# Cutting the 127-row transfers at a sequence's head into 15 and 112 rows, in a backward kernel of two convolutions and a joint network

## The chip, the cores and the metric

The kernel runs on one core of a Trainium2 chip. The time of a run is the device time in microseconds (us). Before the change it was 840.08 us, the median of three runs (835.29 to 840.89). Executions of one kernel scatter here by some 10 us, and a few before runs fell in a slow state (850 to 854 us); comparisons below use the fast runs alone.

Five engines matter. TensorE (PE) multiplies, busy 95% of the span before the change. ScalarE (ACT) and VectorE (DVE) empty its results, busy 88% and 90%. GpSimd (POOL) issues loads through a software queue (on the page of before, q0 software_dynamic, 54.07 MB). SyncE (SP) issues stores and transposing transfers through a hardware queue (q1 hardware_dynamic, 116.45 MB), one after another; "SPq" in a profile is that engine issuing a transfer. The page gives the time of the transfers as a share of 16 DMA engines: 24.9% for q0, 68.2% for q1.

## The reference

```python
def _fwd_reference(x, w1, w2, g, w_f, w_g, w_o):      # x: 2 x 16000 x 256, bf16
    h = gelu(conv(x, w1, K=3))[:, ::2, :]
    f = gelu(conv(h, w2, K=3))[:, ::2, :]             # 2 x 4000 x 256
    fe, ge = f @ w_f, g @ w_g                         # g: 2 x 8 x 256
    j = tanh(fe[:, :, None, :] + ge[:, None, :, :])
    return j @ w_o                                    # 2 x 4000 x 8 x 256

def reference(x, w1, w2, g, w_f, w_g, w_o, grad_out):
    _out, _vjp = jax.vjp(forward, x, w1, w2, g, w_f, w_g, w_o)
    return (_out, *_vjp(grad_out))                    # the output, and a gradient for each input
```

The convolutions are written shorter here than in the original. The output in question is the gradient of x, 2 x 16000 x 256.

## The kernel before

The 2 x 4000 positions after both convolutions are worked off in chunks of up to 512. Four rows of x belong to one position, so a block of 128 positions is stored with 128 partitions of four rows of 256 bf16, 2,048 bytes each. This grid is shifted by three rows against the sequence: the first partition of the first block of a sequence has only one valid row. It is handled alone, and 127 partitions remain.

The two queues, and the helper by which each transfer is issued (all transfers therefore have lines 329 or 331 in a profile; the tile's name tells them apart):

```python
LOADQ, STOREQ = "POOL", "SP"
HR_AT = (0.7, 0.4, 0.3)
    # ... cut ...
    def dma(q, out, in_, r, w, bytes_, new=(), transpose=False, at=None, after=(), cost=None, hold=(), nb=None):
        def go(e):
            eng_ = nc.sync if e == "SP" else nc.gpsimd if e == "POOL" else nc.scalar
            if transpose:
                return eng_.dma_start_transpose(out=out(), in_=in_())
            else:
                return eng_.dma_start(out=out(), in_=in_())
        c = 1260.0 if transpose else 400.0 if q == "SP" else cost or (750.0 if q == "POOL" else 100.0)
        return op(q, c, go, r=r, w=w, new=new, at=at, after=after, hold=hold, nb=nb,
                  work=bytes_ / 256 * 1.25 if transpose else bytes_ / 300.0)
```

The load of x rows for the weight gradient, tile `X` in the profile, from POOL's software queue:

```python
    def load_x5(b, s0, m, at, hold=()):
        X5 = buf("x5", [P, 5, D], BF16, "X5")
        r0, r1 = (1, m) if s0 == 0 else (0, m)
        if s0 + m - 1 == MQ:
            r1 = m - 1
        src = x[b, 0:1, :]
    # ... cut ...
            dma(LOADQ, lambda: X5[:].rearrange("p f d -> p (f d)")[r0:r1],
                lambda: bass.AP(tensor=src.tensor, offset=src.offset + (4 * (s0 + r0) - 3) * D,
                                ap=[[4 * D, r1 - r0], [1, 5 * D]]),
                r=[], w=[(X5, "m")], bytes_=(r1 - r0) * 2560, new=new, at=at, hold=hold, cost=550.0)
        return X5
```

The store of the gradient of x, tile `GX_SB`, on the sync engine's hardware queue:

```python
            s0, m = c0 + bl * P, min(P, Ws - bl * P)
            r0, r1 = (1 if s0 == 0 else 0), (m - 1 if s0 + m - 1 == MQ else m)
            dst = out_1[b, 0:1, :]
            if r0 == 1:
                dma(STOREQ, lambda: out_1[b, 0:1, :], lambda GX=GX: GX[0:1, 3, :], r=[(GX, 1)], w=[], bytes_=512, cost=550.0)
            if r1 > r0:
                dma(STOREQ, lambda s0=s0, r0=r0, r1=r1, dst=dst: bass.AP(
                    tensor=dst.tensor, offset=dst.offset + (4 * (s0 + r0) - 3) * D, ap=[[4 * D, r1 - r0], [1, 4 * D]]),
                    lambda GX=GX, r0=r0, r1=r1: GX[:].rearrange("p c d -> p (c d)")[r0:r1], r=[GX], w=[],
                    bytes_=(r1 - r0) * 2048, cost=550.0)
```

On the same sync queue lie the output's stores (tile `OUT_SB`, six buffers), the transposing loads of `grad_out` (tile `GOT`) and eight transposing copies for each chunk (two each of the tiles `HRo`, `HRs`, `FR` and `HRe`):

```python
    def load_got(g_, u, at):
        b, ci, c0, W = chunks[g_]
        GOT = buf("got", [P, KT, CW], BF16, "GOT")
        dma("SP", lambda: GOT[:, :, :W], lambda: grad_out[b, c0:c0 + W, u, :], r=[], w=[GOT], bytes_=W * D * 2, new=[GOT],
            transpose=True, at=at)
    # ... cut ...
        for kt in range(KT):
            dma("SP", lambda kt=kt: R[:, kt, 0:Wp // P, :], lambda kt=kt: SRC[:, kt, off:off + Wp],
                r=[(SRC, kt)] + [(SRC, k) for k in keys], w=[(R, kt)], bytes_=Wp * P * 2, new=[R] if kt == 0 else [],
                transpose=True, nb=nb)
    # ... cut ...
        late = [start_of[g_] + HR_AT[2] * W] * 2 if g_ < 2 else [t0 + HR_AT[0] * dt, t0 + HR_AT[1] * dt]
        dma_rows("HRo", "hro", g_, HTo, 2, ["z"], late[0])
        dma_rows("HRs", "hrs", g_, HTo, 1, ["h", "z"], late[0])
        dma_rows("HRe", "hre", g_, HTe, 0, ["z"], late[1])
        dma_rows("FR", "fr", g_, FT, 0, ["z"], late[0])
```

PE makes a block of output, ACT or DVE copies it from its accumulator into an `OUT_SB` buffer, the sync queue stores it, and only when the store has landed is the buffer free again; the six are used in turn. A list scheduler with a cost model (`Flow`) fixes the order of instructions on each engine when the kernel is built.

## Time and profile before

| | before |
|---|---|
| three timed runs | 835.29 to 840.89, median 840.08 us |
| profiled run, span | 847.4 us (this run was in the slow state) |
| PE busy | 803.3 us, 95% |
| PE dry in batch 0, at 118.9 us | 8.65 us, then 1.30 |
| 127-row store, batch 1 | holds 15.86 us of the chain |

From the profile's page of before: the span, busy time of each engine with its share and number of instructions, and the engines' shares of the chain of work that ended last.

```profile
span 847.4 us, 17952 instructions
...
PE 803.3 (95%) x6428; PEld 595.2 (70%) x6428; DVE 763.5 (90%) x1730; ACT 749.6 (88%) x1207; POOL 182.6 (22%) x391
...
PE 68%; ACT 12%; DVE 9%; DMA 7%; issue 2%; SPq 1%; ACTq 0%; DVEq 0%; POOL 0%
```

PE is the bound: it is busy 95% of the span and holds 68% of the chain. A change that moves only transfers can gain only where PE waits for something. Two such places have a 127-row store in front of them.

The sync queue's timeline of before in batch 0. Columns: start in us, us that the issue took, engine, line, operation, destination<-source, count.

```profile
102.83 0.75 SPq L331 DMA_DIRECT2D out_dram<-GX_SB  x2
103.67 9.95 SPq L329 DMA_TRANSPOSE GOT<-in_grad_out_dram  x1
113.71 1.11 SPq L331 DMA_DIRECT2D out_dram<-GX_SB  x1
114.88 3.07 SPq L329 DMA_TRANSPOSE HRo<-HTo  x2
118.05 2.70 SPq L329 DMA_TRANSPOSE HRs<-HTo  x2
120.79 3.40 SPq L329 DMA_TRANSPOSE FR<-FT  x2
124.28 0.53 SPq L331 DMA_DIRECT2D out_dram<-OUT_SB  x1
```

The two `GX_SB` stores (1 row and 127 rows) are issued in 0.75 us together. The next instruction is a transpose of `grad_out` (tile `GOT`). The median of the 144 in this profile is issued in 1.27 us; this one holds the queue for 9.95 us, the longest of all. Everything behind it is late, and the next `OUT_SB` store comes only at 124.28.

What the DMA engines did meanwhile, from the stretch table of before. Columns: stretch, its length, busy us and instructions of PE, PEld, DVE, ACT and POOL, granted PE clock, DMA share, GB/s. (The DMA share is a mean over the 16 engines and comes out above 1 in some stretches; only its low, flat values are read here.)

```profile
105.00:110.00 5.00, 5.00 (x37) 3.21 (x36) 4.81 (x11) 5.00 (x10) 0.72 (x1) 1.00 2.34 95
110.00:115.00 5.00, 5.00 (x47) 4.10 (x44) 5.00 (x12) 5.00 (x8) 0.72 (x1) 1.00 0.07 26
115.00:120.00 5.00, 3.93 (x25) 2.21 (x23) 3.09 (x8) 1.08 (x2) 0.57 (x1) 1.00 0.54 167
120.00:125.00 5.00, 0.00 (x0) 0.00 (x0) 0.00 (x0) 0.00 (x0) 0.00 (x0) 0.85 1.30 184
125.00:130.00 5.00, 1.11 (x3) 0.36 (x3) 0.84 (x2) 3.05 (x6) 0.00 (x0) 0.50 0.89 235
```

From 110 to 115 us the core moves 26 GB/s at a DMA share of 0.07, about what one engine of sixteen, busy all the time, would make (an estimate: 1/16 = 0.0625). The next stretches show the consequence: no engine computes from 120 to 125 us, and the granted clock then falls to 0.50.

ACT's and PE's timelines of before, the instructions after the waits ("dry" below means that an engine has nothing that it can start). The brackets give the idle time before an instruction and what ended it.

```profile
126.95 0.58 ACT L314 CAST OUT_SB<-ps 128x512 bf16<-128x512 f32 x1 [10.86 <-DMA out_dram<-OUT_SB]
```

```profile
127.58 1.01 PE L306 MATMUL ps<-GOT,WT 128*128 128x512 bf16 x2 [8.65 <-ACT OUT_SB L314]
129.90 1.01 PE L306 MATMUL ps<-WO,JT 128*128 128x256 bf16 x4 [1.30 <-DVE g_s L436]
```

ACT waits 10.86 us for a store of an `OUT_SB` buffer to land, and PE waits 8.65 us for ACT. In batch 1 the same store shows in the chain of before (start, us, what), and in the list of waits from 500 to 540 us (who waited for what: us, times, longest):

```profile
511.20 15.86 DMA out_dram<-GX_SB
```

```profile
ACT GX_SB L316 <- DMA out_dram<-GX_SB: 4.3, 1, 4.3
...
DVE GX_SB L321 <- DMA out_dram<-GX_SB: 3.0, 1, 3.0
```

There the buffer that runs out is `GX_SB` itself, and the wait is shorter.

### The profile page before, as it was taken

How to read it: one execution, taken by the hardware profiler on the slowest of the kernel's cores; microseconds unless marked ns; L12 is line 12 of the kernel's file. 1: busy time of each engine (PE TensorE's matmuls, PEld its weight loads, DVE VectorE, ACT ScalarE, POOL GpSimd, SP SyncE). 2: the span in 40 equal slices, each digit the busy share in tenths (PEclk: the TensorE clock that was granted, in tenths of full speed). 3: DMA queues.
4: the chain of work that ended last, by engine and by line, in shares of the span. 5: the costliest groups of instructions: out<-in, count | busy, mean ns of one | idle time of the engine just before them, and what ended most of it. 6: DMA issues, size and time to landing. Idle time of an engine off the chain costs nothing.

```text
span 847.4 us, 17952 instructions
## 1 busy us (share of the span) xinstructions
PE 803.3 (95%) x6428; PEld 595.2 (70%) x6428; DVE 763.5 (90%) x1730; ACT 749.6 (88%) x1207; POOL 182.6 (22%) x391
## 2 busy tenths in 40 slices
PE   7589969999999999999999999999999999999995
PEld 5356646677686767877777677576776867788984
DVE  5699958998999989998989998898989999998983
ACT  6789949999899998988899997998898999988762
POOL 5021201212112121233131212112121121214121
PEclk9899998999999999999999999999999999999999
DMA  9989999998979896986899999999999797958452
GB/s 203 162 174 218 213 123 246 248 238 218 249 184 259 199 242 157 237 213 185 200 167 236 230 233 115 221 229 248 210 250 243 182 276 158 255 146 204 107 171 72
DMA packets 330593, 172.05 MB, mean 203 GB/s; under 512 B 275142, under 2 KB 310250, under 8 KB 330504
## 3 DMA queue, kind: packets, MB, share of 16 engines
q1 hardware_dynamic: 313944, 116.45, 68.2%
q0 software_dynamic: 15776, 54.07, 24.9%
q8 instruction: 50, 0.82, 0.4%
q10 hardware_dynamic: 784, 0.39, 0.2%
q14 instruction: 39, 0.32, 0.1%
HBM read 54.44 MB, written 50.34 MB: 124 GB/s over the span
## 4 chain that ended last, share of the span: by engine, by line
PE 68%; ACT 12%; DVE 9%; DMA 7%; issue 2%; SPq 1%; ACTq 0%; DVEq 0%; POOL 0%
PE ps L306 54%; PE GWO L306 10%; PE psb L483 3%; DMA GOT<-in_grad_out_dram 3%; ACT JT L589 2%; DMA out_dram<-GX_SB 2%; ACT JR L609 2%; DVE NGZ L651 2%; ACT JSQ L641 1%; ACT g_sq L432 1%; DVE ZS L659 1%; ACT OUT_SB L314 1%; DVE g_s L436 1%; SPq L329 1%; ACT GX_SB L316 1%
## 5 line engine op out<-in xcount | busy, mean ns | idle before, releaser
L589 ACT ACTIVATE JT<-FE,GE 128x512 bf16<-128x512 bf16 (+2 forms) x288 | 189.1, 696 | 0.7 <-DVE FE L319 0.7
L331 POOL DMA_DIRECT2D GO_R<-in_grad_out_dram x136 | 95.3, 701 | 411.0 <-PE GWO L306 364.6
L306 PE MATMUL ps<-GOT,WT 128*128 128x512 bf16 (+2 forms) x576 | 154.8, 354 | 16.6 <-ACT OUT_SB L314 8.7
L651 DVE SCALAR_TENSOR_TENSOR NGZ<-JSQ,ps 128x512 f32<-128x512 bf16 (+2 forms) x252 | 152.2, 606 | 10.0 <-PE ps L306 9.9
L306 PE MATMUL ps<-WO,JT 128*128 128x256 bf16 x1024 | 154.2, 273 | 2.6 <-DVE g_s L436 1.3
L314 ACT CAST OUT_SB<-ps 128x512 bf16<-128x512 f32 x205 | 127.2, 622 | 19.5 <-DMA out_dram<-OUT_SB 10.9
L609 ACT ACTIVATE JR<-JR 128x1024 bf16<-128x1024 bf16 x128 | 139.1, 1094 | 4.6 <-DVE JR L602 4.3
L306 PEld LDWEIGHTS <-JT 128*128 128x128 bf16 x1024 | 99.7, 98 | 56.8 <-issue 3.3
L306 PE MATMUL GWO<-GO_R,JR 128*128 128x256 bf16 x1024 | 134.1, 274 | 1.3 <-ACT JR L609 1.2
L659 DVE TENSOR_TENSOR ZS<-ZS,NGZ 128x512 f32<-128x512 f32 (+2 forms) x216 | 131.3, 610 | 0.3
L641 ACT ACTIVATE JSQ<-JT 128x1024 bf16<-128x1024 bf16 (+2 forms) x117 | 116.1, 995 | 17.4 <-DVE NGZ L651 17.3
L306 PEld LDWEIGHTS <-WT 128*128 128x128 bf16 x864 | 81.6, 98 | 54.0 <-issue 13.2
L306 PEld LDWEIGHTS <-JR 128*128 128x128 bf16 x1028 | 100.4, 98 | 20.4 <-ACT JR L609 2.4
L306 PEld LDWEIGHTS <-W 128*128 128x128 bf16 x648 | 61.1, 98 | 57.4 <-issue 3.3
L306 PE MATMUL ps<-XC,W 128*128 128x512 bf16 (+2 forms) x432 | 92.2, 351 | 1.7 <-ACT GX_SB L316 1.1
L306 PE MATMUL ps<-ROWS,X 128*128 128x256 bf16 x768 | 92.2, 273 | 0.0
L436 DVE SCALAR_TENSOR_TENSOR g_s<-g_sq,ps 128x512 bf16<-128x512 bf16 (+2 forms) x108 | 66.0, 611 | 27.9 <-ACT HTo L434 14.1
L602 DVE TENSOR_TENSOR JR<-FER,GEB 128x1024 bf16<-128x1024 bf16 x128 | 87.1, 682 | 0.6 <-PE GWO L306 0.5
L306 PEld LDWEIGHTS <-X 128*128 128x128 bf16 x768 | 75.0, 98 | 9.0
L306 PE MATMUL ps<-WT,GHe 128*128 128x256 bf16 x384 | 73.3, 273 | 0.7 <-ACT ROWS L314 0.7
L306 PE MATMUL ps<-WT,GHo 128*128 128x256 bf16 x384 | 73.1, 273 | 0.7 <-ACT GX_SB L316 0.7
L707 DVE TENSOR_TENSOR ACC<-ACC,ps 128x512 f32<-128x512 f32 x96 | 64.1, 678 | 10.5 <-PE ps L306 10.4
(135 smaller groups left out, 1252.7 us busy)
## 6 DMA issues: line engine op xcount, KB each, us to landing
GO_R<-in_grad_out_dram POOLq DMA_DIRECT2D x120, 256.0 KB, 4.6
out_dram<-OUT_SB SPq DMA_DIRECT2D x120, 256.0 KB, 4.4
X<-in_x_dram POOLq DMA_DIRECT2D x60, 320.0 KB, 6.4
out_dram<-GX_SB SPq DMA_DIRECT2D x60, 256.0 KB, 4.9
GOT<-in_grad_out_dram SPq DMA_TRANSPOSE x144, 5.0
out_dram<-g_sq SPq DMA_DIRECT2D x9, 128.0 KB, 1.8
GO_R<-in_grad_out_dram POOLq DMA_DIRECT2D x8, 128.0 KB, 3.2
out_dram<-OUT_SB SPq DMA_DIRECT2D x8, 128.0 KB, 4.6
```

Of the source, the lines that this page charges most:

```text
L306: nc.tensor.matmul(ps_ap, lhsT=lhsT, rhs=rhs, start=start, stop=stop)
L314: nc.scalar.copy(out=dst(), in_=src())
L331: return eng_.dma_start(out=out(), in_=in_())
L436: op("DVE", c_dve(W), lambda e, mt=mt, ps=ps: nc.vector.scalar_tensor_tensor(out=s[:, mt, :W], in0=sq[:, mt, :W], scalar=1.0, in1=ps[:, :W ...
L483: nc.tensor.transpose(out=ps[:m, (bl * KT + kt) * P:(bl * KT + kt + 1) * P], in_=SRC[:, kt, off + bl * P:off + bl * P + m], identity=ident[:])
L589: op("ACT", c_act(W, ptr=True), lambda e, j=j, mt=mt: nc.scalar.activation(out=JT[:, j, mt, :W], in_=S["FE"][:, mt, :W], func=ACT.Tanh, bi ...
L602: op("DVE", c_dve(n * 2 * D, 0.5), lambda e, lo=lo, n=n, m=m, JR=JR: nc.vector.tensor_tensor(out=JR[:m, lo % 2:lo % 2 + n], in0=S["FER"][: ...
L609: op("ACT", c_act(n * 2 * D), lambda e, lo=lo, n=n, m=m, JR=JR: nc.scalar.activation(out=JR[:m, lo % 2:lo % 2 + n], in_=JR[:m, lo % 2:lo % ...
L641: nc.scalar.activation(out=JSQ[:, :, :W], in_=JT[:, j, :, :W], func=ACT.Square)
L651: op("DVE", c_dve(W) + 6, lambda e, d2=d2, ps=ps, u=u, zap=zap, JSQ=JSQ: nc.vector.scalar_tensor_tensor(out=zap(), in0=JSQ[:, d2, :W], sca ...
L659: op("DVE", c_dve(W), lambda e, d2=d2, dst=dst, NGZ=NGZ: nc.vector.tensor_tensor(out=dst[:, d2, :W], in0=ZS[:, d2, :W], in1=NGZ[:, :W], op ...
L707: op("DVE", c_dve(512), lambda e: nc.vector.tensor_tensor(out=acc_ap().rearrange("p k d -> p (k d)"), in0=acc_ap().rearrange("p k d -> p ( ...
```

## The change

The intent is to let the head's transfers run on more DMA engines. In before, the stretch behind the 127-row store has a share of 0.07 and 26 GB/s, while the 60 stores of 128 rows land in 4.9 us in the median, which for their 262,144 bytes is an estimated 53 GB/s. That parts of 15 and 112 rows would be spared the low rate was my assumption; no trace of before shows it. Every row after the first lies in one of the two parts, so no byte is moved twice.

```diff
--- before.py
+++ after.py
@@ -382,6 +382,13 @@
                 bytes_=rem * 1024, at=at, hold=hold)
         st[g_].setdefault("GO", {})[up, h] = GO
 
+    def row_parts(r0, r1):
+
+        cut = (r0 + 15) // 16 * 16
+        parts = [(r0, min(cut, r1)), (min(cut, r1), cut + max(0, r1 - cut) // 16 * 16)]
+        parts += [(parts[-1][1], r1)]
+        return [(lo, hi) for lo, hi in parts if hi > lo]
+
     def load_x5(b, s0, m, at, hold=()):
         X5 = buf("x5", [P, 5, D], BF16, "X5")
         r0, r1 = (1, m) if s0 == 0 else (0, m)
@@ -401,11 +408,12 @@
             dma(LOADQ, lambda: X5[r1:m, 0:3, :],
                 lambda: x[b, 4 * MQ - 3:4 * MQ, :].rearrange("(o f) d -> o f d", o=1),
                 r=[], w=[(X5, "d")], bytes_=1536, at=at, cost=550.0)
-        if r1 > r0:
-            dma(LOADQ, lambda: X5[:].rearrange("p f d -> p (f d)")[r0:r1],
-                lambda: bass.AP(tensor=src.tensor, offset=src.offset + (4 * (s0 + r0) - 3) * D,
-                                ap=[[4 * D, r1 - r0], [1, 5 * D]]),
-                r=[], w=[(X5, "m")], bytes_=(r1 - r0) * 2560, new=new, at=at, hold=hold, cost=550.0)
+        for k, (lo, hi) in enumerate(row_parts(r0, r1)):
+            dma(LOADQ, lambda lo=lo, hi=hi: X5[:].rearrange("p f d -> p (f d)")[lo:hi],
+                lambda lo=lo, hi=hi: bass.AP(tensor=src.tensor, offset=src.offset + (4 * (s0 + lo) - 3) * D,
+                                             ap=[[4 * D, hi - lo], [1, 5 * D]]),
+                r=[], w=[(X5, ("m", k))], bytes_=(hi - lo) * 2560, new=new, at=at, hold=hold, cost=550.0)
+            new = []
         return X5
 
     def load_g(q, at):
@@ -843,11 +851,11 @@
             dst = out_1[b, 0:1, :]
             if r0 == 1:
                 dma(STOREQ, lambda: out_1[b, 0:1, :], lambda GX=GX: GX[0:1, 3, :], r=[(GX, 1)], w=[], bytes_=512, cost=550.0)
-            if r1 > r0:
-                dma(STOREQ, lambda s0=s0, r0=r0, r1=r1, dst=dst: bass.AP(
-                    tensor=dst.tensor, offset=dst.offset + (4 * (s0 + r0) - 3) * D, ap=[[4 * D, r1 - r0], [1, 4 * D]]),
-                    lambda GX=GX, r0=r0, r1=r1: GX[:].rearrange("p c d -> p (c d)")[r0:r1], r=[GX], w=[],
-                    bytes_=(r1 - r0) * 2048, cost=550.0)
+            for lo, hi in row_parts(r0, r1):
+                dma(STOREQ, lambda s0=s0, lo=lo, hi=hi, dst=dst: bass.AP(
+                    tensor=dst.tensor, offset=dst.offset + (4 * (s0 + lo) - 3) * D, ap=[[4 * D, hi - lo], [1, 4 * D]]),
+                    lambda GX=GX, lo=lo, hi=hi: GX[:].rearrange("p c d -> p (c d)")[lo:hi], r=[GX], w=[],
+                    bytes_=(hi - lo) * 2048, cost=550.0)
             if r1 < m:
                 dma(STOREQ, lambda: out_1[b, 4 * MQ - 3:4 * MQ, :].rearrange("(o f) d -> o f d", o=1),
                     lambda GX=GX, r1=r1, m=m: GX[r1:m, 0:3, :], r=[GX], w=[], bytes_=1536, cost=550.0)
```

The order of instructions on PE, DVE and ACT stays the same. On the sync and POOL queues two issues are added each. On the sync queue one 128-row `GX_SB` store of batch 0 also moves behind six row transposes, because the scheduler's cost model sees different times.

## The prediction, made before the result was known

> **What bounds the kernel.** By the chain that ended last, TensorE holds 68% of the span (847.4 us in the profiled run), ScalarE 12%, VectorE 9%, DMA 7%. PE is busy 803.3 us, DVE 763.5, ACT 749.6 (busy table): from about 135 to 435 us and from 556 us on PE runs without gaps; time is lost where PE is starved. The change touches two such places.
>
> **Stall 1 (batch 0).** The sync queue's timeline shows the 1-row and 127-row grad-x stores issued at 102.8 to 103.6 us. The next instruction, a GOT transpose normally issued in 1.25 us, holds the queue 9.95 us and lands after 16.9. The stretch table shows DMA at a flat 25 to 27 GB/s and 0.06 to 0.07 share from 110 to 117 us: one engine of sixteen. 127 rows x 2,048 B at 26.5 GB/s is an estimated 9.8 us, which fits. [...] Everything behind it in the ring waits: the OUT_SB store the evacuations need is issued only at 124.28 and lands at 126.87. ACT idles 10.86 us, DVE 11.07, PE 8.65 and then 1.30; PE's granted clock falls to 0.5, so its first work after takes about 2.4 us too long.
>
> **Stall 2 (batch 1).** The same store at 511.2 us lands after 15.3 us and holds 15.86 us of the chain, with 25 to 27 GB/s again from 522 to 529 us. But compute has slack: ACT idles 4.3 us and DVE 3.0 for the grad-x buffer (waits list), PE 3 to 4 us in pieces.
>
> **What the change does.** Per batch one store becomes a 15-row and a 112-row one, one load likewise: four more issues in all (about 0.4 us each on the sync queue, 0.55 on POOL, which is 22% busy). Bytes stay. The instruction order of PE, DVE and ACT is unchanged; on the sync queue one 128-row grad-x store of batch 0 moves behind six row transposes. The 112-row store should land like the 128-row ones, median 4.9 us. With the GOT transpose issued in 1.3 us, the OUT_SB store goes out 9 to 10 us earlier, landing near 117 us, before PE runs dry at 118.9.
>
> The load halves should give nothing: the first 127-row load landed in 12.8 us, but so did the 128-row load beside it (13.1), the second in under 8 us, and no PE wait names X. The early GOT wait (7.4 us of PE) is start-up traffic and stays.
>
> **Sum.** Stall 1: 8.65 + about 1 + 2.4 = 12 us, on PE's critical path. Stall 2: 3 to 4 us. Together about 15.5 us, 1.8%: from 840.1 to 824.5 us. Range 815 to 834. Chances: faster by over 2% 0.36, within 2% 0.62, slower 0.02.
>
> **What would show it right.** No stretch at 26 GB/s near 106 to 117 or 522 to 529 us; the GOT transpose after the stores issued in under 2.5 us; no ACT wait for DMA OUT_SB above 2 us; PE clock 1.0 from 120 to 135 us; the grad-x store's share of the chain falling from 2.1% towards 0; PE idle down 12 to 14 us; X loads landing as before.
>
> **What would make it wrong.** The split store might still crowd few engines (832). Stall 2's slack may be taken by ACT and DVE, near full there (1 us instead of 4). The timed runs, 7 us shorter, may stall differently. The earlier transfers could collide with other traffic (DMA is at 90% share). If the loads also sat on one engine, the start-up wait shrinks too and the gain passes 2%.

## The result, and the profile after

The changed kernel takes 827.42 us (median of six fast runs, 827.24 to 829.04); before was run six times in the same rounds, median 839.6. The ratio is 0.9867, with a 95% interval of 0.9842 to 0.9891. Ratios here are the mean time of one kernel's fast runs over that of the other's of the same rounds (827.72 over 838.88), so not quite the ratio of the medians; for the experiments see the note below their table. The kernel is 1.3% faster, which is within the 2% that counts as the same.

The first profile of before is of a slow run and must not be subtracted from a fast one. So before was profiled again (run `before_again` below). That run took 842.0 us, span 839.9. The first of the two places in it, from its sync queue, stretch table, ACT and PE timelines:

```profile
94.86 0.77 SPq L331 DMA_DIRECT2D out_dram<-GX_SB  x2
95.72 11.35 SPq L329 DMA_TRANSPOSE GOT<-in_grad_out_dram  x1
...
117.72 0.53 SPq L331 DMA_DIRECT2D out_dram<-OUT_SB  x1
```

```profile
104.00:106.00 2.00, 1.97 (x19) 1.72 (x18) 2.00 (x6) 2.00 (x4) 0.14 (x1) 1.00 0.07 27
```

```profile
120.60 0.59 ACT L314 CAST OUT_SB<-ps 128x512 bf16<-128x512 f32 x1 [10.87 <-DMA out_dram<-OUT_SB]
```

```profile
121.23 1.01 PE L306 MATMUL ps<-GOT,WT 128*128 128x512 bf16 x2 [8.72 <-ACT OUT_SB L314]
123.56 1.01 PE L306 MATMUL ps<-WO,JT 128*128 128x256 bf16 x4 [1.31 <-DVE g_s L436]
```

The stall is the same in the fast state: a hold of 11.35 us, a rate of 27 GB/s at a share of 0.07, an ACT wait of 10.87 us, a PE wait of 8.72 us, then 1.31. Now after, first its page:

```profile
span 825.8 us, 17958 instructions
...
PE 799.4 (97%) x6428; PEld 593.6 (72%) x6428; DVE 763.4 (92%) x1730; ACT 749.2 (91%) x1207; POOL 182.0 (22%) x393
...
PE 69%; ACT 13%; DVE 10%; DMA 4%; issue 2%; SPq 2%; ACTq 0%; DVEq 0%; POOL 0%
```

The sync queue of after at the same instructions:

```profile
92.78 2.36 SPq L331 DMA_DIRECT2D out_dram<-GX_SB  x3
95.24 1.32 SPq L329 DMA_TRANSPOSE GOT<-in_grad_out_dram  x1
96.60 2.58 SPq L329 DMA_TRANSPOSE HRo<-HTo  x2
...
105.18 0.39 SPq L331 DMA_DIRECT2D out_dram<-OUT_SB  x1
```

The three stores are issued in 2.36 us, and the transpose behind them in 1.32 us. The 15-row part lands in 3.9 us, the 112-row part in 5.6. The `OUT_SB` store goes out at 105.18, 12.4 us after the head's stores; in the second profile of before that was 117.72 - 94.86 = 22.9 us. Two stretches of after, with the columns as before, and the instructions after ACT's and PE's waits:

```profile
95.00:100.00 5.00, 5.00 (x39) 3.27 (x38) 4.77 (x10) 5.00 (x9) 1.00 (x3) 1.00 1.09 257
...
110.00:115.00 5.00, 3.58 (x22) 2.04 (x21) 3.19 (x9) 4.98 (x9) 0.00 (x0) 1.00 1.20 245
```

```profile
110.02 0.59 ACT L314 CAST OUT_SB<-ps 128x512 bf16<-128x512 f32 x1 [1.59 <-DMA out_dram<-OUT_SB]
```

```profile
112.98 0.60 PE L306 MATMUL ps<-WO,JT 128*128 128x256 bf16 x4 [1.30 <-DVE g_s L444]
```

The flat stretch near 26 GB/s is gone, ACT's wait fell to 1.59 us, PE's wait for `OUT_SB` is gone, and its clock stays 1.00. The 1.30 us wait for `g_s` is left. In batch 1 the list of waits of after, from 480 to 530 us, has no wait for a `GX_SB` buffer. (In the second profile of before ACT waited 3.01 us there for such a buffer, until 519.65 us. The profile puts this down to PE and does not record when the 127-row store landed. But the wait ended 15.0 us after the issue of the head's stores began, at 504.63, and the core moved 25 to 27 GB/s from 514 to 520 us; in the first profile the store ended ACT's wait 15.9 us after its issue. So the store is the likelier cause there too, but this is not shown.)

To see how much each place gave, the start of the same instruction is compared in both fast profiles:

| instruction | second profile of before | after | difference |
|---|---|---|---|
| PE, before batch 0's head | 70.54 | 69.61 | 0.93 |
| PE, after stall 1 | 177.77 | 166.62 | 11.15 |
| PE, before batch 1's head | 468.80 | 457.64 | 11.16 |
| PE, after stall 2 | 549.10 | 534.66 | 14.44 |
| end of the span | 839.9 | 825.8 | 14.1 |

Stall 1 gave 11.15 - 0.93 = 10.2 us and stall 2 gave 14.44 - 11.16 = 3.3. Nothing moved in the 290 us between. The 0.93 us before the first head could not be traced to the split. The pair of profiles differs by 14.1 us and the means of the timed runs by 11.2: the profiled run of before, 842.0, was itself 3.1 us above its kernel's mean in the first comparison.

These are two profiles only. The same instructions can be found in all 13 fast profiles of this document, those of the experiments below included. Batch 0's head (first to second row of the table) took 98.4 to 111.4 us in the five kernels with a 127-row or 113-row store on a hardware queue at the heads, and 95.3 to 98.9 in the eight with the head's stores split into 15 and 112 rows, or with the whole store on the software queue. Batch 1's head (third to fourth row) took 78.2 to 83.3 us in those five, and 77.0 to 77.3 in these eight. Batch 1's head separates the kernels cleanly. Batch 0's head scatters by several us from run to run, so 10.2 us is what one pair shows.

### The profile page after: what moved, and what is told of

Read it like the earlier page. It is cut to its first block, busy times and chain, and to the rows that moved or that the text cites. A ratio compares the mean times of both kernels' runs of the same rounds, so it can differ in the third digit from the quotient of the medians.

```text
span 825.8 us, 17958 instructions
## 1 busy us (share of the span) xinstructions
PE 799.4 (97%) x6428; PEld 593.6 (72%) x6428; DVE 763.4 (92%) x1730; ACT 749.2 (91%) x1207; POOL 182.0 (22%) x393
## 3 DMA queue, kind: packets, MB, share of 16 engines
q0 software_dynamic: 15840, 54.07, 23.9%
## 4 chain that ended last, share of the span: by engine, by line
PE 69%; ACT 13%; DVE 10%; DMA 4%; issue 2%; SPq 2%; ACTq 0%; DVEq 0%; POOL 0%
PE ps L306 55%; PE GWO L306 10%; PE psb L491 4%; ACT JT L597 3%; ACT JR L617 2%; DVE NGZ L659 2%; ACT OUT_SB L314 2%; ACT JSQ L649 2%; SPq L329 2%; ACT g_sq L440 2%; DVE ZS L667 1%; DVE g_s L444 1%; ACT g_s L450 1%; DMA W<-in_w_dram 1%; DMA out_dram<-g_sq 1%
## 5 line engine op out<-in xcount | busy, mean ns | idle before, releaser
L659 DVE SCALAR_TENSOR_TENSOR NGZ<-JSQ,ps 128x512 f32<-128x512 bf16 (+2 forms) x252 | 155.3, 619 | 2.5 <-PE ps L306 2.4
L314 ACT CAST OUT_SB<-ps 128x512 bf16<-128x512 f32 x205 | 126.7, 619 | 10.2 <-PE ps L306 8.5
L667 DVE TENSOR_TENSOR ZS<-ZS,NGZ 128x512 f32<-128x512 f32 (+2 forms) x216 | 134.0, 623 | 0.3
L649 ACT ACTIVATE JSQ<-JT 128x1024 bf16<-128x1024 bf16 (+2 forms) x117 | 115.8, 993 | 11.6 <-DVE NGZ L659 11.2
L610 DVE TENSOR_TENSOR JR<-FER,GEB 128x1024 bf16<-128x1024 bf16 x128 | 88.9, 696 | 0.6 <-PE GWO L306 0.5
```

The source lines that it names most:

```text
L314: nc.scalar.copy(out=dst(), in_=src())
L610: op("DVE", c_dve(n * 2 * D, 0.5), lambda e, lo=lo, n=n, m=m, JR=JR: nc.vector.tensor_tensor(out=JR[:m, lo % 2:lo % 2 + n], in0=S["FER"][: ...
L649: nc.scalar.activation(out=JSQ[:, :, :W], in_=JT[:, j, :, :W], func=ACT.Square)
L659: op("DVE", c_dve(W) + 6, lambda e, d2=d2, ps=ps, u=u, zap=zap, JSQ=JSQ: nc.vector.scalar_tensor_tensor(out=zap(), in0=JSQ[:, d2, :W], sca ...
L667: op("DVE", c_dve(W), lambda e, d2=d2, dst=dst, NGZ=NGZ: nc.vector.tensor_tensor(out=dst[:, d2, :W], in0=ZS[:, d2, :W], in1=NGZ[:, :W], op ...
```

## The experiments

My theory: on the hardware queue the 127-row store runs on one DMA engine (my reading of the share of 0.07), the sync queue behind it is held for about 10 us, and the buffers behind the queue run out. Rivals: the sync queue's new order does it; two smaller pieces do it, whatever their row counts; the loads' split does it; the store only needs to leave the sync queue. All kernels gave correct results.

| run | timed median (range) | ratio to before [95%] |
|---|---|---|
| before_again | 842.24 (838.25 to 845.6) | 1.0036 [0.9998, 1.0075] |
| stores_only | 831.28 (827.81 to 833.79) | 0.9905 [0.9872, 0.9937] |
| loads_only | 836.72 (832.29 to 838.52) | 0.9961 [0.9928, 0.9994] |
| stores_prime | 838.51 (831.98 to 841.7) | 0.9994 [0.9960, 1.0027] |
| after_again | 830.57 (827.38 to 836.41) | 0.9870 [0.9822, 0.9918] |
| stores_only_2 | 829.65 (827.96 to 834.57) | 0.9854 [0.9814, 0.9895] |
| loads_all_127 | 834.56 (828.54 to 836.95) | 0.9897 [0.9844, 0.9949] |
| before_store_pool | 830.77 (826.49 to 834.76) | 0.9861 [0.9809, 0.9914] |
| before_store_act | 842.83 (839.59 to 848.41) | 1.0045 [0.9998, 1.0092] |
| after_plus_one | 832.23 (827.23 to 837.38) | 0.9910 [0.9861, 0.9959] |
| before_late | 846.95 (844.38 to 851.89) | 1.0084 [1.0041, 1.0126] |
| after_late | 828.15 (827.09 to 831.51) | 0.9867 [0.9825, 0.9909] |

The first four runs share one chip and its runs of before (fast mean 839.45), the next four another (842.37), the last four a third (840.01). The ratios come out of the listed times when before's first run is left out, and for stores_prime, after_again and after_late the profiled run too. With all fast runs stores_prime would have 837.42 / 839.45 = 0.9976, inside its interval; the others move by 0.0005 at most.

### before_again: the unchanged kernel

> The kernel before, unchanged, for a second profile and the scatter of its times. The first profile had a start-up wait of TensorE for a GOT transpose of 7.42 us, which the profile of the changed kernel has as 1.02 us. If that wait is the state of that one execution, this profile should be of about 840 us or less, with a start-up wait of 1 to 2 us, and still with the 8.65 us wait near 120 us and the 15.86 us of the chain near 511 us. If the wait belongs to the unsplit load, it is there again with 6 to 8 us. Ratio to before 1.000 within 0.3 per cent.

The unchanged kernel against itself came out at 1.0036, an interval that just holds 1. So differences of 0.4% are not to be read here. Its profile is the one used above.

### stores_only and stores_only_2: the loads unsplit

```diff
-        for k, (lo, hi) in enumerate(row_parts(r0, r1)):
+        for k, (lo, hi) in enumerate([(r0, r1)]):
```

> Only the stores are split, the loads stay at 127 rows. Theory (the 127-row store sits on one DMA engine and holds everything behind it in the same ring; the loads never did): the same time as the full change, ratio to before 0.985 to 0.989, X landing as before, start-up wait as in the other runs. Rival (part of the gain is the load, which also sat on one engine and made the start-up wait): ratio 0.992 to 0.996, and the start-up wait for GOT is 5 us or more.

> Only the stores split, repeated. In the first call its runs fell into two groups, 828 to 830 and 833 to 834 us, and the ratio was 0.9905. If the loads matter, the upper group is there again, ratio 0.989 to 0.992. If the upper group was scatter of that call, ratio 0.985 to 0.988 like the full change.

The first time the ratio was 0.9905, which left 0.4% that the loads might have given. So it was repeated beside the full change: 0.9854 against 0.9870. The stores' split alone gives the whole gain that these runs can resolve. The first difference reads as scatter: the six stores_only runs fell into two clusters, near 828 and near 833 us.

### loads_only: the stores unsplit

```diff
-            for lo, hi in row_parts(r0, r1):
+            for lo, hi in [(r0, r1)]:
```

> Only the loads are split, the stores stay at 127 rows. Theory: no gain, ratio 0.998 to 1.002, both stretches at 25 to 27 GB/s still there, TensorE idle 8 to 9 us near 120 us. Rival (the load matters): ratio 0.991 to 0.996 with a start-up wait of 1 us where the kernel before has 7.

The ratio 0.9961 barely excludes 1. The mechanism of before is back, as its sync queue shows:

```profile
92.31 9.90 SPq L329 DMA_TRANSPOSE GOT<-in_grad_out_dram  x1
```

The transpose behind the store held the queue 9.90 us, the DMA engines moved 25 to 27 GB/s from 98 to 106 us, and PE waited 4.47 us for `OUT_SB`. A small gain from the loads can't be excluded by this run; the pair above shows none.

### stores_prime: the same number of pieces, cut at another row

```diff
-            for lo, hi in row_parts(r0, r1):
+            for lo, hi in ([(r0, 15), (15, r1)] if r0 == 1 else row_parts(r0, r1)):
```

The store is cut into 14 and 113 rows. The order of all instructions is that of the full change.

> As the full change, but the store is cut into 14 and 113 rows in place of 15 and 112: the same number of issues, the same bytes, the same order of all instructions, and nearly the same sizes[...]. Theory [...]: the 113-row part runs on one engine, an estimated 113 x 2048 B / 26.5 GB/s = 8.7 us, so a stretch at 25 to 27 GB/s comes back and the following GOT transpose holds the sync queue 7 to 9 us; most of the gain is lost, ratio 0.995 to 1.000. Rivals (smaller pieces help by themselves, or the gain is the new order on the sync queue, where one grad x store stands behind six transposes): the same as the full change, ratio 0.985 to 0.989.

The gain is gone, as far as the runs resolve it: 0.9994 [0.9960, 1.0027]. Its sync queue, and a stretch in which the DMA engines had the queue's work:

```profile
88.87 1.17 SPq L331 DMA_DIRECT2D out_dram<-GX_SB  x3
90.14 9.87 SPq L329 DMA_TRANSPOSE GOT<-in_grad_out_dram  x1
```

```profile
98.00:100.00 2.00, 2.00 (x14) 1.17 (x13) 1.98 (x5) 2.00 (x6) 0.35 (x2) 1.00 0.06 26
100.00:102.00 2.00, 2.00 (x17) 1.40 (x15) 1.82 (x4) 2.00 (x5) 0.01 (x1) 1.00 0.07 26
```

The hold is back at 9.87 us, and so is the low rate, 26 GB/s at a share of 0.06 to 0.07. This kills two rivals at once: order and number of pieces were those of the full change, and only the row counts differed. What sets 113 and 127 rows apart from 112 is not shown. One caution: this profile comes from the kernel's fastest run (831.98 us), in which PE lost only 0.43 us to `OUT_SB`. The hold was there, but the buffers lasted longer. In batch 1 its head took 78.2 us, between the 77.0 of after and the 80.3 of the second profile of before. See "How long the buffers last" below.

### after_again, loads_all_127: the loads, turned up

> The full change once more, beside the store-only kernel on one chip, to settle whether the split of the loads is worth anything. Full change: ratio to before 0.985 to 0.988, runs within 827 to 830 us. If the loads matter, the store-only kernel of this call is 2 to 4 us slower than this one in the mean; if they do not, the two agree within 1 us.

The full change repeated on another chip: 0.9870, as the first time (0.9867).

In loads_all_127 the stores are split as in the change, and every 128-row load of x is cut into 127 rows and 1, on POOL's software queue:

```diff
-        for k, (lo, hi) in enumerate(row_parts(r0, r1)):
+        for k, (lo, hi) in enumerate([(0, 127), (127, 128)] if (r0, r1) == (0, P) else [(r0, r1)]):
```

> The dose for the loads: the full change for the stores, but every 128-row x load of the steady state is cut into 127 and 1 rows, on the software queue as before, and the loads at the heads are left at 127. Theory (a software-queue load of 127 rows is spread over the engines): the 127-row loads land in 5 to 7 us like the 128-row ones, no stretch at 26 GB/s, time within 1 per cent of the full change (830 to 838 us; 60 more issues on POOL). Rival (127 rows sit on one engine here too, 325 KB at 26.5 GB/s, an estimated 12.3 us each, 62 times): the loads land in 12 us or more and the time is over 860 us.

Its list of DMA issues, the 127-row loads (count, size, median us to landing):

```profile
X<-in_x_dram POOLq DMA_DIRECT2D x62, 317.5 KB, 7.2
```

62 loads of 127 rows land in 7.2 us in the median, against 6.4 for the 128-row loads of before. 325,120 bytes at the 26 GB/s of the flat stretches would take an estimated 12.5 us. So these 127-row loads from the software queue did not run at that rate: 7.2 us makes an estimated 45 GB/s. (The two unsplit loads at the heads agree in the second profile of before: 7.3 us; in the slow first one it was 12.8.) The ratio, 0.9897, overlaps that of the full change; 60 extra one-row loads may cost something, but these four runs don't show it.

### before_store_pool: the unsplit store on the software queue

```diff
-    def dma(q, out, ..., nb=None):
+    def dma(q, out, ..., nb=None, via=None):
         def go(e):
+            e = via or e
@@ the head's store, 127 rows as before @@
-                    bytes_=(r1 - r0) * 2048, cost=550.0)
+                    bytes_=(r1 - r0) * 2048, cost=550.0, via="POOL" if r0 == 1 else None)
```

> The kernel before with one thing changed: the unsplit 127-row store is issued from POOL on the software queue instead of the sync queue, at the same place in the order. Theory (only a hardware queue puts 127 rows on one engine): the store lands in about 5 to 7 us, no stretch at 26 GB/s, stall 1 and 2 gone, ratio 0.986 to 0.992. Rival (127 rows sit on one engine on any queue): a stretch at 26 GB/s remains, the store lands after 10 us or more, and the time falls less, ratio 0.993 to 1.000.

127 rows in one piece, at the same place of the program's order, give the full gain: 0.9861. From the list of DMA issues of this run:

```profile
out_dram<-GX_SB POOLq DMA_DIRECT2D x2, 254.0 KB, 4.0
```

The 254 KB land in 4.0 us, and PE no longer waits for `OUT_SB` in batch 0. At the 26 GB/s of the flat stretches its 260,096 bytes would take an estimated 10.0 us. So it is not the number 127 that costs here, but 127 rows on the sync engine's hardware queue. (Two things changed at once: the store also left the sync queue, and in batch 0 it went out at 79.66 us, as soon as the block was ready and 13 us before the 1-row store. Whether the landing time depends on that was not tested; for the time gained, the next run is the control. The sync queue keeps before's order here, so the gain does not need the new order either.)

### before_store_act: the unsplit store on another hardware queue

The same edit with `via="ACT"`: the store is issued from ACT's hardware queue (q10 hardware_dynamic, 0.91 MB here and 0.39 in before) and leaves the sync queue. (The edit adds a line to the helper, so L329 is L330 here.)

> The kernel before, but the unsplit 127-row store is issued from ACT, on the other hardware ring, at the same place in the order[...]. Told apart: is it the place in the sync queue's ring that holds the transposes, or is it the one engine being busy? Ring: the GOT transpose behind the stores is issued in under 3 us, the OUT_SB store goes out in time, TensorE loses under 3 us near 120 us, ratio 0.985 to 0.991, and the store itself still needs 10 us or more to land. Engine: the GOT transpose is held 8 us or more as before, ratio 0.996 to 1.002.

The ratio is 1.0045: nothing gained. The sync queue and a stretch of this run:

```profile
88.15 4.59 SPq L330 DMA_TRANSPOSE GOT<-in_grad_out_dram  x1
...
94.58 5.85 SPq L330 DMA_TRANSPOSE GOT<-in_grad_out_dram  x1
```

```profile
90.00:95.00 5.00, 5.00 (x36) 3.42 (x35) 3.16 (x7) 4.59 (x8) 1.03 (x3) 0.97 1.32 72
95.00:100.00 5.00, 5.00 (x33) 3.04 (x31) 4.68 (x11) 5.00 (x9) 1.66 (x3) 1.00 1.40 64
```

The store was not on the sync queue, and yet two transposes on it took 4.59 and 5.85 us to issue. That alone proves little: the median of the 144 is 1.28 us, but in after, with no such store, the longest took 5.36. The rate says more. In stretches of 10 us from 30 to 720 us, only two of this run moved less than 100 GB/s, one at each head: 68 GB/s from 90 to 100 us and 62 from 510 to 520. In after no such stretch moved less than 107. Against a usual 1.25 us the queue loses (4.59 - 1.25) + (5.85 - 1.25) = 7.9 us in two pieces, where it lost 8.7 and 10.1 us in one piece in the two profiles of before. So a low rate, 68 and 62 GB/s, came at both heads, and in batch 0 two slow transposes with it, though the store was on another queue. That the store is what slowed them is an inference: no profile tells the engines apart.

The run is no clean test, though, and neither alternative came as I had written it: the holds stayed under 8 us, and the time did not fall. In batch 0 ACT itself stood 4.25 us around the issue (the profile puts this down to an `OUT_SB` store), and PE 3.43 us at 87.23 us; after that the big `OUT_SB` stall did not come (PE waited 0.29 us at 118.80). By the PE instructions of the table above, batch 0's head took 101.1 us (107.2 in the second profile of before, 97.0 in after) and batch 1's head 83.3 us (80.3 and 77.0). So leaving the sync queue gave part of the first stall back and lost more at the second, where the transposes `HRo` and `HRs` held the sync queue 8.17 and 6.26 us (two issues each) and PE waited 2.81 us for `GX_SB`. That it is not enough to leave the sync queue is shown by batch 1's head in this one profile; the timed ratio agrees, but ACT's own wait is in it. Batch 0's head stays 4.1 us behind that of after; how much of this is the store's transfer and how much is ACT's own wait is not separated.

### after_plus_one: one 127-row store in the steady state

```diff
-            for lo, hi in row_parts(r0, r1):
+            for lo, hi in ([(0, 127), (127, 128)] if (g_, bl) == (4, 0) else row_parts(r0, r1)):
```

The full change, with one 128-row store in the middle of batch 0 cut into 127 rows and 1.

> The dose for the stores: the full change, plus one 128-row grad x store in the middle of batch 0 (fifth chunk, first block) cut into 127 and 1 rows on the sync queue, so that a single one-engine store falls into the steady state. Theory: the next transpose is held about 10 us and a stretch at 25 to 27 GB/s appears there; the stall that follows costs 4 to 10 us, ratio to before 0.992 to 1.000 where the full change has 0.987. Rival (only the heads of the sequences are short of slack, the steady state hides 10 us): the stretch is there, but the time stays that of the full change, ratio 0.985 to 0.988.

The mechanism came as expected, with a shorter hold. The sync queue and a stretch:

```profile
272.63 4.34 SPq L331 DMA_DIRECT2D out_dram<-GX_SB  x3
277.06 6.92 SPq L329 DMA_TRANSPOSE GOT<-in_grad_out_dram  x1
```

```profile
282.00:284.00 2.00, 2.00 (x19) 1.60 (x18) 1.90 (x5) 2.00 (x3) 0.00 (x0) 1.00 0.38 26
284.00:286.00 2.00, 2.00 (x21) 1.80 (x19) 0.00 (x0) 2.00 (x5) 0.00 (x0) 1.00 0.07 26
```

A transpose is held 6.92 us (about 10 was expected), and the core moves 26 GB/s from 282 to 286 us. The cost is another matter: PE loses 1.00 us, at 307 us, and by the same instructions in both profiles (166.62 to 457.64 in after, 167.07 to 459.56 here) about 1.5 us. This is less than the 4 to 10 us that I expected and more than nothing. The timed intervals of this kernel and of the full change overlap, so the runs don't settle how much it is. The same store at another place costs another amount. My reading is that a hold of 7 to 11 us becomes a stall only where the buffers run out sooner; this profile does not measure how long they would have lasted.

### before_late and after_late: taking the work behind the store out of its way

At a head, the held queue still has six row transposes to do before the `OUT_SB` store that ACT needs. In before_late these six, for that chunk alone, come later; the 127-row store stays whole. In after_late the same is done to the full change.

```diff
-        late = [...] * 2 if g_ < 2 else [t0 + HR_AT[0] * dt, t0 + HR_AT[1] * dt]
+        late = [...] * 2 if g_ < 2 else [t0 + (1.2 if g_ == 2 else HR_AT[0]) * dt, t0 + HR_AT[1] * dt]
```

> The kernel before with the 127-row stores as they are, but the six row transposes of one chunk (the third of batch 0), which stand in the sync queue between the held GOT transpose and the OUT_SB store, are moved behind the next OUT_SB stores. The order on all other engines is the same. If stall 1 is the sum of the held transpose (about 10 us) and those six (about 9 us) ahead of the OUT_SB store, then the store goes out about 9 us earlier, ACT's wait for it falls from 10.9 us to 1 to 3 us, TensorE loses 0 to 1 us there, and stall 2 stays: ratio 0.988 to 0.993, although the one-engine stretch is still there. If the one engine itself is what starves the compute engines, the stall stays 8 to 9 us and the ratio is 0.998 to 1.002.

I had expected a gain of about 1%. Half of the expectation held: the `OUT_SB` stall went (ACT waited 1.74 us, PE not at all for `OUT_SB`), though the hold was still there. But the kernel got slower, 1.0084, and the reason is further on. The hold, on the sync queue, and the new wait, on ACT's and PE's timelines:

```profile
94.59 10.37 SPq L329 DMA_TRANSPOSE GOT<-in_grad_out_dram  x1
...
141.40 1.57 SPq L331 DMA_DIRECT2D out_dram<-GX_SB  x1
```

```profile
153.07 0.60 ACT L316 ACTIVATE GX_SB<-ps 128x512 bf16<-128x512 f32 x1 [14.22 <-DMA out_dram<-GX_SB]
```

```profile
153.72 1.29 PE L306 MATMUL ps<-NGFE,WT 128*128 128x512 bf16 x2 [10.90 <-ACT GX_SB L316]
```

A later, ordinary 128-row `GX_SB` store, issued at 141.40 and landing 11.6 us later, now made ACT wait 14.22 us and PE 10.90.

> The full change with the same move of six row transposes, which should take away what was left of stall 1 (ACT waited 1.4 to 1.6 us for the OUT_SB store, TensorE 1.1 to 1.3 us for what hung on it). Expected: that wait gone, 1 to 2 us less than the full change, ratio 0.983 to 0.987; with the scatter of the last call this may not be resolved. If the moved transposes come too late for the weight gradients, a new wait of TensorE for HRo, HRs or FR appears and the time is the same or worse.

With the split and the same move this wait does not appear: 0.9867, the same as the full change without the move. So the order alone doesn't make it; it needs the 127-row store too. The reading is that the queue carries its debt on until some buffer runs out. The two sync timelines show the debt: at the head's stores this queue is 3.6 us behind that of after_late (93.88 and 90.25), at the first moved transpose 10.0 us (122.67 and 112.68), and at the `GX_SB` store 9.5 us (141.40 and 131.95). The order of the queue is the same in both but for the split, and PE's instruction before the head starts within 0.3 us (71.23 and 71.47). That this debt made ACT's wait is an inference from the pair. In the profile of after_late the last 1.3 us wait of the full change is gone (span 826.1). But it is gone in the profile of after_plus_one too, whose order at this head is that of the full change, so the move is not shown to have removed it. The time is not better (828.15). No version that I ran beats the full change clear of the noise (the lowest ratios, 0.9854 and 0.9861, have it within their intervals).

### How long the buffers last

How large stall 1 is depends on how far ahead of ACT the sync queue was. Four profiles with a hold and the usual order, and one of the full change, from the sync and ACT timelines: the time from the head's store to the moment when ACT runs dry, and the wait that follows.

| kernel | store issued | ACT dry | lead | ACT's wait | sum |
|---|---|---|---|---|---|
| before (slow) | 102.83 | 116.09 | 13.3 | 10.86 | 24.1 |
| before_again | 94.86 | 109.73 | 14.9 | 10.87 | 25.7 |
| loads_only | 91.61 | 108.5 | 16.9 | 6.64 | 23.5 |
| stores_prime | 88.87 | 110.2 | 21.3 | 2.63 | 23.9 |
| after | 92.78 | 108.43 | 15.65 | 1.59 | 17.2 |

With a 127-row or 113-row store the sum is 24 to 26 us each time, so what varies most is the lead: 13 to 21 us. The split shortens the sum to 17 in after (14.7 in after_again and 15.4 in stores_only). So one profile alone can over- or understate the gain. The varying lead may also be a reason why the timed runs with a whole store scatter. I did not test that, and it cannot be the only one: after_again has no whole store, and its six runs range from 827.38 to 836.41. What sets the lead in a given run is open.

## Why the prediction was right or wrong

The time, 827.42 us, lies in the predicted range (815 to 834), 2.9 us above the predicted 824.5, and the most likely class, within 2%, came. The range would have held any gain from 6 to 25 us, so the parts say more than the hit.

- **The bound and the mechanism** were right. A 127-row store on the hardware queue ran at 25 to 27 GB/s and a share of 0.06 to 0.07 in the flat stretches (26 GB/s again for 113 rows), held the queue about 10 us, and starved ACT and then PE. The split removed the hold (transpose 1.32 us; under 2.5 was predicted), the 26 GB/s stretch, ACT's wait (1.59; at most 2) and the lost clock (1.00).
- **Stall 1, "8.65 + about 1 + 2.4 = 12 us"**, was mis-sized. It measured 10.2 in the pair of fast profiles. The first term held (8.72). The second did not: the 1.30 us wait for `g_s` is still there in after, unchanged. It is no fixed cost of either kernel: after_again (1.10) and stores_only (1.31) have it, while stores_only_2, before_store_pool, after_plus_one and after_late don't. The third was too large: 10.2 - 8.72 leaves 1.5 us for the lost clock and everything else. The half clock was real, from about 117 to 127 us in the second profile of before, but it cost less than I had counted. The stretch table of this profile shows where: from 120 to 124 us, at clock 0.50, PE was busy only 1.46 of 4 us, so it was mostly waiting anyway. Only from 124 us on did it work without a gap, 2 us at 0.50 and 2 us at 0.67, which makes an estimated 1.0 + 0.7 = 1.7 us lost. PE was dry from 112.5 us, and its clock was 1.00 up to 116 us, 0.77 in the stretch from 116 to 118 and 0.50 after. In after, with its wait of 1.30 us, the clock was 1.00 in every stretch from 110 to 130 us.
- **Stall 2, "3 to 4 us"**, was right: 3.3.
- **The loads "should give nothing"**: right as far as the runs resolve it (0.9854 without, 0.9870 with the loads' split). Their landing times scatter more than the split could change them: the largest part of such a load took 12.8 us in the slow profile of before, 7.3 in the fast one and 10.7 after.
- **The early wait for GOT, 7.4 us, "stays"**: wrong, and for a plain reason. It belonged to the slow run that I had read. In the fast profiles it was 1.69 us before and 1.02 after.
- **The store's share of the chain, "from 2.1% towards 0"**, was a poor sign. The second profile of before doesn't list that store in its chain at all, though the same stalls are in it. Which chain is listed varies from one profile to the other.
- **"PE idle down 12 to 14 us"** cannot be checked well. Span less PE's busy time was 44.1 us in the slow profile of before, 42.9 in the fast one, from which 93 of PE's records are missing, and 26.4 after.
- **The sum**: 15.5 us were predicted, and the fast pair of profiles shows 10.2 + 3.3 = 13.5 us at the two heads. The timed means differ by 11.2. The rest lies within the scatter of the runs: the profiled run of before was 3.1 us above its mean.

## What to carry to other kernels

Look for stretches in which the DMA rate is flat and low (here a share of 0.06 to 0.07, and 25 to 27 GB/s), and check the row counts of the hardware-queue transfers issued just before. Here 127 rows gave such a stretch; cut into 15 and 112 they did not (ratio 0.9867), cut into 14 and 113 they did (0.9994), and issued whole from the software queue they landed in 4.0 us (0.9861). No other split of the head's store was tried. Judge the cost by the first buffer that runs out behind the slow transfer, not by the transfer itself: it was about 10 us at one place, 3.3 and about 1.5 at others, and moving other work out of the held queue's way removed one stall and brought another. Before subtracting two profiles, make sure that both runs were in the same state.
